# An mLSTM cell followed by a gated MLP: the first chunk's loads, masks and conversions are rearranged

## The chip, the cores and the metric

The kernel runs on one NeuronCore of a Trainium2 chip. The time is the device time of one execution in microseconds (us). The median of the kernel before is 486.15 us, of three runs between 485.81 and 486.62.

A core has five engines that run their own instruction streams and wait for each other through semaphores: TensorE (in the profile PE, and PEld for its weight loads), VectorE (DVE), ScalarE (ACT), GpSimd (POOL) and SyncE (SP), which here mostly issues loads. Matrix products land in PSUM; VectorE and ScalarE read it from there, GpSimd[...] only touches SBUF, the on-chip memory.

## The reference

There are 4 batches with 8 heads, a sequence of 768 and a head size of 40. Per head a matrix state `C` and a vector state `n` are updated at each step, with gates that are stabilised by a running maximum `m`; the output of all heads is one row of 320 numbers for a two-layer MLP.

```python
for t in range(S):
    m_new  = np.maximum(f_gate[:, :, t] + m, i_gate[:, :, t])
    f_stab = np.exp(f_gate[:, :, t] + m - m_new)
    i_stab = np.exp(i_gate[:, :, t] - m_new)
    m = m_new
    C = f_stab * C + i_stab * outer(v_t, k_t)
    n = f_stab * n + i_stab * k_t
    y[:, :, t] = sigmoid(o_t) * (C @ q_t) / np.maximum(np.abs(n @ q_t), 1.0)
x = y.transpose(0, 2, 1, 3).reshape(3072, 320)
h = x @ w_in                                  # 320 -> 2048
out = (h * sigmoid(1.702 * h)) @ w_out        # 2048 -> 320
```

## The kernel before

The sequence is cut into six chunks of 128 steps. Within a chunk the recurrence becomes a masked product: scores `k q`, times a weight `exp(a_s - m_t)` that is zero where s comes after t, times the values. Chunk 0 has no earlier state, so its attention begins as soon as keys, queries and gates are on the chip. While it runs, the weights `w_in` and `w_out` are loaded in 20 pieces (each 512 columns) and converted from their stored form by ScalarE ("A") and VectorE ("V"). Then the MLP of a chunk runs beside the attention of the next one.

The order of the loads, all issued by SyncE; `fetch(n)` loads piece n:

```python
def load_gates(w):
    for dst, src in ((f_sb, f_gate), (i_sb, i_gate)):
        dst[w] = ld.tile([BH, L], FP, tag="fi", bufs=4, name="fi")
        nc.sync.dma_start(out=dst[w], in_=src[:, :, w * L:(w + 1) * L].rearrange("b h s -> (b h) s"))

load_gates(0)
for what, n in (("kq", 0), ("kq", 1), (load_gates, 1), ("vo", 0), ("vo", 1), ("kq", 2), (fetch, 0), ("kq", 3),
                (fetch, 1), ("vo", 2), ("vo", 3), *((fetch, n) for n in range(2, 10))):
    ...
```

TensorE begins with dummy products, so that its array is busy until the first keys come; two buffers are cleared on ScalarE:

```python
def keep_busy(n, pool=ps_a, tag="a"):
    p_idle = pool.tile([128, W], FP, tag=tag, name="p_idle")
    for _ in range(n):
        T.matmul(p_idle, idle, idle.unsqueeze(1).to_broadcast([128, 4, 128]), start=True, stop=True)

keep_busy(8, ps_m, "m")
...
for t in (k_bl.rearrange("p j g c -> p (j g c)"), state.rearrange("p j a b -> p (j a b)")):
    A.copy(out=t, in_=idle[:, 0:1].to_broadcast(t.shape))
```

The conversion of a piece, the transposes of keys and queries, the weights and the scores of chunk 0. `ps_a` is a ring of four PSUM banks. `not_yet` holds -1e30 where s comes after t, and the first product of each bank adds it:

```python
def convert(n, engines="AV"):
    lo, hi, dst = bits[n][:, :, 0], bits[n][:, :, 1], pieces[n][0]
    dst_u = dst.bitcast(U32)
    if "A" in engines:
        A.activation(out=dst, in_=hi.bitcast(FP), func=AF.Abs)
        A.activation(out=lo, in_=lo, func=AF.Copy, scale=2.0 ** -29)
    if "V" not in engines:
        return
    V.tensor_scalar(...); V.tensor_scalar(...); V.scalar_tensor_tensor(...); V.tensor_tensor(...)   # cut

def transposes(w, b, which=slice(0, 2)):
    for bl, st, dst, name in ((k_bl, k_st, kT, "kT"), (q_bl, q_st, qT, "qT"))[which]:
        ...
        pt = ps_a.tile([128, NP, L], FP, tag="a", name="p_t")
        for p in range(NP):
            T.transpose(pt[:, p, :], st[:, h:h + 2, :]..., ident)
        if b == 0:
            keep_busy(1)
        A.copy(out=dst[w, b], in_=pt)

def weights(w, b):
    if w == 0:
        x = wt[w, b] = work.tile([L, NP, 2, L], FP, tag="wt", bufs=4, name="wt")
        for i in range(2):
            pw = ps_a.tile([L, NP, L], FP, tag="a", name="p_w")
            T.matmul(pw, ident_bf, not_yet.unsqueeze(1).to_broadcast([L, NP, L]), start=True, stop=False)
            for p in range(NP):
                h = b * H + 2 * p + i
                one = pick[:, h:h + 1].to_broadcast([3 * BH, L])
                T.matmul(pw[:, p, :], one, m3, start=False, stop=False)
                T.matmul(pw[:, p, :], a3, one, start=False, stop=(p == NP - 1))
            A.activation(out=x[:, :, i, :], in_=pw, func=AF.Exp)
        return
    ...

def scores(w, b):
    pw = [pool.tile([L, NP, L], FP, tag=tag, name="p_s") for _ in range(2)]      # pool: ps_a in chunk 0
    ...                                                                          # 8 products into two banks
    for i in range(2):
        V.tensor_tensor(out=wt[w, b][:, :, i, :], in0=pw[i], in1=wt[w, b][:, :, i, :], op=OP.mult)
```

The first chunk's sequence:

```python
gates(0)
...
transposes(0, 0)
weights(0, 0)
transposes(0, 1)
gates(1)
scores(0, 0)
weights(0, 1)
scores(0, 1)
gate_out(0); gate_out(1)
values(0, 0); values(0, 1)
transposes(0, 2)
convert(0, "A")
weights(0, 2)
seam(0, 0); seam(0, 1)
convert(0, "V")
scores(0, 2)
convert(1, "A")
transposes(0, 3)
weights(0, 3)
convert(1, "V")
scores(0, 3)
columns(0)
gate_out(2); gate_out(3)
scale(0, 0); scale(0, 1)
values(0, 2, states=True); values(0, 3, states=True)
full_rows(0, 0, 0); full_rows(1, 0, 0)      # first products with w_in, pieces 0 and 1
convert(2, "A")                             # piece 2: the last 64 rows of w_in, hidden blocks 0 to 3
seam(0, 2); full_rows(0, 1, 0); seam(0, 3); full_rows(1, 1, 0)
convert(2, "V")
convert(3)
convert(4)
...                                         # more full_rows, then the products with w_in_x (piece 2)
```

`seam` transposes a batch's output rows for the MLP, `gate_out` applies the output gate's tanh, `values` multiplies the weights by the values.

Of the kernel before, what the change touches and what calls it, by code (L numbers as in the profile page):

```python
# [12 lines left out]
OP = mybir.AluOpType  # L13
# [9 lines left out]
L = 128  # L23
# [11 lines left out]
def kernel(  # L35
# [12 lines left out]
    nc = tc.nc  # L48
    B, H, S, D = q.shape
# [4 lines left out]
    NP = H // 2  # L54
# [39 lines left out]
    def load_gates(w):  # L94
        for dst, src in ((f_sb, f_gate), (i_sb, i_gate)):
            dst[w] = ld.tile([BH, L], FP, tag="fi", bufs=4, name="fi")
            nc.sync.dma_start(out=dst[w], in_=src[:, :, w * L:(w + 1) * L].rearrange("b h s -> (b h) s"))

    def load(w, what, bs=slice(0, B)):
        hs = slice(bs.start * H, bs.stop * H)  # L100
# [66 lines left out]


    load_gates(0)
    for what, n in (("kq", 0), ("kq", 1), (load_gates, 1), ("vo", 0), ("vo", 1), ("kq", 2), (fetch, 0), ("kq", 3),  # L170
                    (fetch, 1), ("vo", 2), ("vo", 3), *((fetch, n) for n in range(2, 10))):
        if isinstance(what, str):
            load(0, what, slice(n, n + 1))
        else:
            what(n)
# [9 lines left out]
    def keep_busy(n, pool=ps_a, tag="a"):  # L185
        p_idle = pool.tile([128, W], FP, tag=tag, name="p_idle")
        for _ in range(n):
            T.matmul(p_idle, idle, idle.unsqueeze(1).to_broadcast([128, 4, 128]), start=True, stop=True)

    keep_busy(8, ps_m, "m")  # L190
    ident = const.tile([128, 128], FP, name="ident")
    make_identity(nc, ident)
    one1 = const.tile([BH, 1], FP, name="one1")
# [16 lines left out]
    a3 = const.tile([3 * BH, L], BF, name="a3")  # L210
    m3 = const.tile([3 * BH, L], BF, name="m3")
    state = const.tile([128, BH // 2, 2, D1], FP, name="state")
    for t in (k_bl.rearrange("p j g c -> p (j g c)"), state.rearrange("p j a b -> p (j a b)")):
        A.copy(out=t, in_=idle[:, 0:1].to_broadcast(t.shape))

    t1, t2, t4 = (const.tile([128, NH, DH], FP, name=f"t{i}") for i in (1, 2, 4))

# [2 lines left out]
    kT, qT, wt, ys, xT, gs, o_ps, p_c = {}, {}, {}, {}, {}, {}, {}, {}  # L220


    def convert(n, engines="AV"):

        lo, hi, dst = bits[n][:, :, 0], bits[n][:, :, 1], pieces[n][0]
        dst_u = dst.bitcast(U32)
        if "A" in engines:
            A.activation(out=dst, in_=hi.bitcast(FP), func=AF.Abs)
# [3 lines that stand above are left out]
        V.tensor_scalar(out=dst, in0=dst, scalar1=HI_MIN, scalar2=HI_MAX, op0=OP.max, op1=OP.min)  # L232
        V.tensor_scalar(out=dst_u, in0=dst_u, scalar1=3, scalar2=0x3FFFFFFF, op0=OP.logical_shift_left,
                        op1=OP.bitwise_and)
        V.scalar_tensor_tensor(out=dst_u, in0=hi, scalar=0xC0000000, in1=dst_u, op0=OP.bitwise_and,
                               op1=OP.bitwise_or)
        V.tensor_tensor(out=dst_u, in0=dst_u, in1=lo, op=OP.add)
# [59 lines left out]
    def transposes(w, b, which=slice(0, 2)):  # L297
        for bl, st, dst, name in ((k_bl, k_st, kT, "kT"), (q_bl, q_st, qT, "qT"))[which]:
            dst[w, b] = work.tile([128, NP, L], FP, tag=name, bufs=4, name=name)
            if w:  # L300
                V.transpose(out=dst[w, b].rearrange("p j t -> p (j t)"),
                            in_=bl[:, b * NP:(b + 1) * NP].rearrange("p j g c -> p (j g c)"))
                continue
            pt = ps_a.tile([128, NP, L], FP, tag="a", name="p_t")
            for p in range(NP):
                h = b * H + 2 * p
                T.transpose(pt[:, p, :], st[:, h:h + 2, :].rearrange("p a b -> p (a b)"), ident)
# [4 lines that stand above are left out]
    def spread(w):  # L312

        for b in range(B):
            x = wt[w, b] = work.tile([L, NP, 2, L], FP, tag="wt", bufs=4, name="wt")
            nc.sync.dma_start(out=x.rearrange("s p i t -> s (p i) t"),
                              in_=m_row[w][b * H:(b + 1) * H, :].unsqueeze(0).to_broadcast([L, H, L]))

    def weights(w, b):
        if w == 0:  # L320
            x = wt[w, b] = work.tile([L, NP, 2, L], FP, tag="wt", bufs=4, name="wt")
            for i in range(2):
                pw = ps_a.tile([L, NP, L], FP, tag="a", name="p_w")
                T.matmul(pw, ident_bf, not_yet.unsqueeze(1).to_broadcast([L, NP, L]), start=True, stop=False)
                for p in range(NP):
                    h = b * H + 2 * p + i
                    one = pick[:, h:h + 1].to_broadcast([3 * BH, L])
                    T.matmul(pw[:, p, :], one, m3, start=False, stop=False)
                    T.matmul(pw[:, p, :], a3, one, start=False, stop=(p == NP - 1))
                A.activation(out=x[:, :, i, :], in_=pw, func=AF.Exp)  # L330
            return
        x = wt[w, b].rearrange("s p i t -> s (p i) t")
        for h in range(H):
            A.activation(out=x[:, h, :], in_=x[:, h, :], func=AF.Exp, scale=-1.0,  # L334
                         bias=cols[w][:, b * H + h:b * H + h + 1])
        G.affine_select(out=x, in_=x, compare_op=OP.is_ge, fill=0.0, base=0, pattern=[[0, H], [1, L]],  # L336
                        channel_multiplier=-1)
        if w > 1 and b == 0:
            gates_out(w)

# [13 lines left out]
    def values(w, *bs, states=False):  # L354
        po, pi = {}, {}
        for b in bs:
            po[b] = ps_a.tile([L, H, D1], FP, tag="a", name="p_o")
            for p in range(NP):
                for i in range(2):
                    h = 2 * p + i  # L360
                    for t in HALVES:
                        T.matmul(po[b][t, h, :], wt[w, b][:, p, i, t], v_st[:, b * H + h, :], start=True, stop=True)
        for b in bs if w else ():
            pi[b] = ps_a.tile([L, H, D1], FP, tag="a", name="p_i")
            for p in range(NP):
                for t in HALVES:
                    T.matmul(pi[b][t, 2 * p:2 * p + 2, :].rearrange("p a b -> p (a b)"), qT[w, b][:, p, t],
                             state[:, b * NP + p].rearrange("p a b -> p (a b)"), start=True, stop=True)
        if states:
            for b in bs:  # L370
                scale_values(w, b)
        if states and w == 1:
            for b in bs:
                scale_state(w, b)
        elif states and w:

            new_states(w)
            for b in bs:
                scale_state(w, b)
        for b in bs:  # L380
            u = po[b]
            if w:
                u = work.tile([L, H, D1], FP, tag="u", name="u")
                g = cols[w][:, BH + b * H:BH + (b + 1) * H].unsqueeze(2).to_broadcast([L, H, D1])
                V.tensor_tensor(out=u, in0=pi[b], in1=g, op=OP.mult)
                V.tensor_tensor(out=u, in0=po[b], in1=u, op=OP.add)

            den = work.tile([L, H, 1], FP, tag="den", name="den")
            V.tensor_scalar(out=den, in0=u[:, :, D:D1], scalar1=-1.0, scalar2=1.0, op0=OP.mult, op1=OP.max)
            V.tensor_tensor(out=den, in0=u[:, :, D:D1], in1=den, op=OP.max)  # L390
            V.reciprocal(out=den, in_=den)
            z = eo[w][:, b * H:(b + 1) * H, :]
            V.scalar_tensor_tensor(out=z, in0=z, scalar=1.0, in1=u[:, :, 0:D], op0=OP.add, op1=OP.mult)
            y = ys[w, b] = work.tile([L, DM + 64], FP, tag="y", name="y")
            V.scalar_tensor_tensor(out=y[:, 0:DM].rearrange("p (h d) -> p h d", d=D), in0=z, scalar=0.5,
                                   in1=den.to_broadcast([L, H, D]), op0=OP.mult, op1=OP.mult)
            G.tensor_copy(out=y[:, DM:DM + 64], in_=y[:, DM - 64:DM])
# [21 lines left out]
    def scale(w, b):  # L419
        scale_values(w, b)  # L420
        scale_state(w, b)
# [238 lines left out]
    def gate_out(b):  # L660
        z = eo[0][:, b * H:(b + 1) * H, :]
        A.activation(out=z, in_=z, func=AF.Tanh, scale=0.5)
# [11 lines left out]
    V.tensor_reduce(out=pair, in_=ident[0:BH, 0:BH].rearrange("p (j two) -> p j two", two=2), axis=AX.X, op=OP.add)  # L674
    V.tensor_copy(out=half[0:BH], in_=par.unsqueeze(2).to_broadcast([BH, 2, 64]))
    transposes(0, 0)
    weights(0, 0)
    transposes(0, 1)
    gates(1)
    scores(0, 0)  # L680
    weights(0, 1)
    scores(0, 1)
    gate_out(0)
    gate_out(1)
    values(0, 0)
    values(0, 1)
    transposes(0, 2)
# [11 lines left out]
    columns(0)  # L699
    gate_out(2)  # L700
    gate_out(3)
    scale(0, 0)
    scale(0, 1)

# [16 lines left out]
    full_rows(0, 1, 0)  # L721
    seam(0, 3)
    full_rows(1, 1, 0)
    convert(2, "V")
    convert(3)
    convert(4)
    for j in range(2):
        for c in range(2):
            full_rows(j, c, 1)
# [132 lines left out]
```

## Time and profile before

| what | us |
|---|---|
| median time (three runs) | 486.15 |
| span of the profiled execution | 486.1 |
| TensorE busy | 480.6 |
| VectorE busy | 342.7 |
| ScalarE busy | 221.0 |
| GpSimd busy | 60.3 |
| first load issued | 0.81 |
| first transposes of keys start on TensorE | 5.02 |
| first scores start | 11.40 |
| first product with piece 2 of `w_in` starts | 36.17 |

A row of the order of time has the start, the duration (of the group from its first start to its last end), the engine, the line of the kernel, the operation, and what it writes and reads; a bracket tells how long the engine was idle before it, and what released it. A row of the table of stretches has each engine's busy time in that stretch. Ends of matrix products are modelled, so the durations of neighbours overlap, and the spacing of starts tells the pace better than a duration does.

### The profile page before, as it was taken

What the parts mean: (1) busy time and instruction counts of PE and PEld (TensorE: products, weight loads), DVE (VectorE), ACT (ScalarE), POOL (GpSimd) and SP (SyncE); (2) the same over time, 40 slices, a digit from 0 to 9 for tenths busy, and PEclk for the clock granted to TensorE, in tenths of its full rate; (3) what the DMA queues carried; (4) which work ended last, traced back from release to release, by engine and by line L of the source; (5) the groups of instructions that cost most, each with busy time, mean ns of one, the idle gap of its engine ahead of it and who ended that gap; (6) DMA issues with size and microseconds to landing.
All of it is one profiled execution on the core that took longest, in us unless ns stands there. A gap on an engine that the chain in (4) does not pass through costs nothing. (4 is left out here: it accounts for less than half of the span.)

```text
span 486.1 us, 10432 instructions
## 1 busy us (share of the span) xinstructions
PE 480.6 (99%) x4072; PEld 398.2 (82%) x4072; DVE 342.7 (70%) x853; ACT 221.0 (45%) x575; POOL 60.3 (12%) x101
## 2 busy tenths in 40 slices
PE   8999999999999999999999999999999999999997
PEld 5884457777779999787999877999977999977997
DVE  7798878887978965667766686696576786254831
ACT  6666764603559401467700465900364920255300
POOL 3020002520000430000331000232000120000000
DMA  8999589963996100997100796300393000000000
GB/s 121 188 270 347 66 202 188 171 81 70 169 202 73 11 28 30 155 209 80 8 29 1 119 253 75 32 28 3 77 261 28 1 14 17 28 1 0 1 27 28
DMA packets 175953, 44.87 MB, mean 92 GB/s; under 512 B 164352, under 2 KB 169504, under 8 KB 175904
## 3 DMA queue, kind: packets, MB, share of 16 engines
q1 hardware_dynamic: 175328, 43.55, 48.3%
q8 instruction: 32, 0.52, 0.5%
q10 hardware_dynamic: 576, 0.66, 0.4%
q14 instruction: 17, 0.14, 0.1%
HBM read 40.17 MB, written 4.01 MB: 91 GB/s over the span
## 5 line engine op out<-in xcount | busy, mean ns | idle before, releaser
L615 PE MATMUL p_out<-w_out_sb,g 128*128 128x160 f32 x480 | 69.8, 301 | 0.0
L615 PEld LDWEIGHTS p_out<-w_out_sb,g 128*128 128x128 f32 x480 | 66.3, 190 | 1.0
L405 ACT COPY xT<-p_x 128x384 f32<-128x384 f32 x24 | 10.8, 483 | 120.7 <-PE p_x L404 107.6
L526 DVE TENSOR_TENSOR g<-p_u,g 128x256 f32<-128x256 f32 x80 | 33.7, 425 | 44.6 <-PE p_u L518 35.0
L523 ACT COPY g<-p_u 128x256 f32<-128x256 f32 x120 | 43.1, 377 | 43.5 <-PE p_u L518 39.3
L530 ACT ACTIVATE g<-g 128x256 f32<-128x256 f32 x120 | 42.4, 425 | 39.7 <-DVE g L526 39.7
L336 POOL TENSOR_SCALAR_AFFINE_SELECT wt<-wt 128x1024 f32<-128x1024 f32 x20 | 22.8, 1138 | 239.3 <-ACT wt L334 236.9
L620 DVE TENSOR_TENSOR o_sb<-o_sb,p_out 128x160 f32<-128x160 f32 x70 | 21.4, 318 | 42.2 <-PE p_out L615 41.8
L334 ACT ACTIVATE wt<-wt,cols 128x128 f32<-128x128 f32 x160 | 47.9, 392 | 0.0
L518 PE MATMUL p_u<-xT,w_in_sb 128*128 128x256 f32 x160 | 38.9, 382 | 0.0
L518 PE MATMUL p_u<-xs,big 128*128 128x256 f32 x160 | 37.9, 379 | 0.0
L352 DVE TENSOR_TENSOR wt<-p_s,wt 128x512 f32<-128x512 f32 x48 | 30.4, 684 | 9.4 <-POOL wt L336 6.7
L546 PE MATMUL p_u<-xT,w_in_x 64*128 64x512 f32 x80 | 37.0, 602 | 0.0
L546 PE MATMUL p_v<-xT,w_in_x 64*128 64x512 f32 x80 | 37.0, 602 | 0.0
L566 PE MATMUL p_out<-w_out_sb,g 128*128 128x320 f32 x128 | 36.3, 436 | 0.0
L615 PE MATMUL p_out<-t,big 128*128 128x160 f32 x240 | 35.5, 301 | 0.0
L518 PEld LDWEIGHTS p_u<-xT,w_in_sb 128*128 128x128 f32 x160 | 29.6, 190 | 5.4 <-DVE o_sb L620 1.5
L518 PEld LDWEIGHTS p_u<-xs,big 128*128 128x128 f32 x160 | 30.0, 190 | 4.6 <-ACT g L523 0.2
L615 PEld LDWEIGHTS p_out<-t,big 128*128 128x128 f32 x240 | 33.3, 190 | 0.2
L566 PEld LDWEIGHTS p_out<-w_out_sb,g 128*128 128x128 f32 x128 | 23.8, 190 | 9.8 <-issue 0.5
L526 DVE TENSOR_TENSOR g<-p_v,g 128x256 f32<-128x256 f32 x80 | 29.9, 415 | 0.0
L546 PEld LDWEIGHTS p_v<-xT,w_in_x 64*128 64x128 f32 x80 | 14.2, 186 | 16.4 <-issue 16.0
(172 smaller groups left out, 862.0 us busy)
## 6 DMA issues: line engine op xcount, KB each, us to landing
wt<-m_row SPq DMA_DIRECT2D x20, 512.0 KB, 7.0
v_st<-in_v_dram SPq DMA_DIRECT2D x5, 640.0 KB, 8.9
eo<-in_o_gate_dram SPq DMA_DIRECT2D x5, 640.0 KB, 5.8
k_st<-in_k_dram SPq DMA_DIRECT2D x5, 640.0 KB, 11.4
out_dram<-o_sb SPq DMA_DIRECT2D x20, 160.0 KB, 1.8
big<-in_moe_w_in_dram SPq DMA_DIRECT2D x5, 512.0 KB, 6.8
k_bl<-in_k_dram SPq DMA_DIRECT2D x40, 64.0 KB, 2.8
q_bl<-in_q_dram SPq DMA_DIRECT2D x40, 64.0 KB, 2.8
```

Of the source, the lines that this page charges most:

```text
L334: A.activation(out=x[:, h, :], in_=x[:, h, :], func=AF.Exp, scale=-1.0, bias=cols[w][:, b * H + h:b * H + h + 1])
L336: G.affine_select(out=x, in_=x, compare_op=OP.is_ge, fill=0.0, base=0, pattern=[[0, H], [1, L]], channel_multiplier=-1)
L352: V.tensor_tensor(out=wt[w, b][:, :, i, :], in0=pw[i], in1=wt[w, b][:, :, i, :], op=OP.mult)
L405: A.copy(out=xT[w][:, :, b, :], in_=px)
L518: T.matmul(p[k][:, ts[t]], a[:, k // 2, k % 2 * 128:(k % 2 + 1) * 128], b, start=first, stop=True, skip_group_check=True)
L523: A.copy(out=g[k][i][:, ts[t]], in_=chain[k][:, ts[0]])
L526: V.tensor_tensor(out=g[k][i][:, ts[t]], in0=p[k][:, ts[pt]], in1=g[k][i][:, ts[t]], op=OP.add)
L530: A.activation(out=dst, in_=dst if src is None else src, func=AF.Gelu_apprx_sigmoid)
L546: T.matmul(p[k], w_in_x[r, k, :], x[r, 2, :], start=False, stop=True, skip_group_check=True)
L566: T.matmul(po, gs[w, f // 2][:, f % 2, b * L:(b + 1) * L], w_out_sb[:, f, :], start=(f == 0), stop=(f == NF - 1))
L615: T.matmul(po, a(f), b[:, f, :], start=(f == 0), stop=(f == NH - 1))
L620: V.tensor_tensor(out=dst, in0=x, in1=po, op=OP.add)
```

## The change

The gates of chunks 0 and 1 are loaded from ScalarE's queue, ahead of everything else there, so that SyncE's queue begins with the keys. One dummy product is left out. The clears of the two buffers leave the front of ScalarE's queue for later places. The keys of batch 1 are transposed before the weights of batch 0, to give TensorE work while the gates are computed. For batches 0 and 1 the mask is no longer added by TensorE: GpSimd writes zeros into the finished weights. Piece 2 (the 64 rows left over of `w_in`) is converted by VectorE in two halves, the second after pieces 3 and 4.

```diff
     def load_gates(w):
...
-            nc.sync.dma_start(out=dst[w], in_=src[:, :, w * L:(w + 1) * L].rearrange("b h s -> (b h) s"))
+            (nc.sync if w > 1 else nc.scalar).dma_start(
+                out=dst[w], in_=src[:, :, w * L:(w + 1) * L].rearrange("b h s -> (b h) s"))
...
     load_gates(0)
-    for what, n in (("kq", 0), ("kq", 1), (load_gates, 1), ("vo", 0), ("vo", 1), ("kq", 2), (fetch, 0), ("kq", 3),
+    load_gates(1)
+    for what, n in (("kq", 0), ("kq", 1), ("vo", 0), ("vo", 1), ("kq", 2), (fetch, 0), ("kq", 3),
...
-    keep_busy(8, ps_m, "m")
+    keep_busy(7, ps_m, "m")
...
-    for t in (k_bl.rearrange("p j g c -> p (j g c)"), state.rearrange("p j a b -> p (j a b)")):
+    def clear(t):
         A.copy(out=t, in_=idle[:, 0:1].to_broadcast(t.shape))
...
-    def convert(n, engines="AV"):
-        lo, hi, dst = bits[n][:, :, 0], bits[n][:, :, 1], pieces[n][0]
+    def convert(n, engines="AV", part=slice(0, 512)):
+        lo, hi, dst = bits[n][:, part, 0], bits[n][:, part, 1], pieces[n][0][:, part]
...
+    def causal(x, n):
+        G.affine_select(out=x, in_=x, compare_op=OP.is_ge, fill=0.0, base=0, pattern=[[0, n], [1, L]],
+                        channel_multiplier=-1)
...
-                T.matmul(pw, ident_bf, not_yet.unsqueeze(1).to_broadcast([L, NP, L]), start=True, stop=False)
+                if b > 1:
+                    T.matmul(pw, ident_bf, not_yet.unsqueeze(1).to_broadcast([L, NP, L]), start=True, stop=False)
...
-                    T.matmul(pw[:, p, :], one, m3, start=False, stop=False)
-                    T.matmul(pw[:, p, :], a3, one, start=False, stop=(p == NP - 1))
+                    T.matmul(pw[:, p, :], one, m3, start=(b < 2), stop=False)
+                    T.matmul(pw[:, p, :], a3, one, start=False, stop=(b < 2 or p == NP - 1))
                 A.activation(out=x[:, :, i, :], in_=pw, func=AF.Exp)
+                if b < 2:
+                    causal(x[:, :, i, :], NP)
...
     transposes(0, 0)
+    transposes(0, 1, slice(0, 1))
     weights(0, 0)
-    transposes(0, 1)
+    transposes(0, 1, slice(1, 2))
...
     gate_out(1)
+    clear(k_bl.rearrange("p j g c -> p (j g c)"))
...
     gate_out(3)
+    clear(state.rearrange("p j a b -> p (j a b)"))
...
-    convert(2, "V")
+    convert(2, "V", slice(0, 256))
     convert(3)
     convert(4)
+    convert(2, "V", slice(256, 512))
```

More of the change, by code (lines that the diff above doesn't have):

```diff
@@ L335, in weights @@
                          bias=cols[w][:, b * H + h:b * H + h + 1])
-        G.affine_select(out=x, in_=x, compare_op=OP.is_ge, fill=0.0, base=0, pattern=[[0, H], [1, L]],
-                        channel_multiplier=-1)
+        causal(x, H)
         if w > 1 and b == 0:
```

## The prediction

> **What bounds the kernel now.** First the page's busy shares, then the kernel cut into stretches of time, then TensorE's own order of time at the start, its waits, and the load queue.
>
> The page's first part, per engine busy us (share) and instructions:
>
> ```profile
> PE 480.6 (99%) x4072; PEld 398.2 (82%) x4072; DVE 342.7 (70%) x853; ACT 221.0 (45%) x575; POOL 60.3 (12%) x101
> ```
>
> TensorE (PE) has work for 480.6 of 486.1 us, so any gain must come out of the stretch where it is idle or doing work that the result doesn't need. The table of stretches says where that is:
>
> ```profile
> core 0: us, PE busy (x) PEld busy (x) DVE busy (x) ACT busy (x) POOL busy (x), PEclk, DMA share, GB/s
> 0.00:5.00 5.00, 3.60 (x8) 1.05 (x9) 3.64 (x13) 4.19 (x3) 2.89 (x12) 1.00 0.46 73
> 5.00:10.00 5.00, 4.91 (x24) 3.38 (x25) 3.80 (x16) 1.92 (x4) 1.72 (x5) 1.00 1.22 152
> ...
> 20.00:25.00 5.00, 4.64 (x50) 3.74 (x50) 4.54 (x9) 4.91 (x11) 0.00 (x0) 1.00 0.88 172
> 25.00:30.00 5.00, 4.97 (x88) 4.42 (x89) 4.62 (x13) 2.65 (x7) 2.91 (x5) 1.00 0.93 229
> ...
> 100.00:150.00 50.00, 49.91 (x361) 38.47 (x360) 41.09 (x93) 19.89 (x56) 3.48 (x7) 1.00 0.77 129
> ```
>
> In the first 5 us PE runs only eight dummy matmuls; after 30 us it is never idle for more than 0.1 us in a stretch until the tail. The DMA column shows the loads saturated (about 1) from 5 us. So the change, which touches only the first chunk, moves the point at which the dense stretch begins; if later stages can follow, the whole kernel shifts by that. TensorE's order of time (start, duration, line, and the idle time before it):
>
> ```profile
> 1.06 3.60 PE L188 MATMUL p_idle<-idle 128*128 128x512 bf16 x8 [1.06 <-DVE idle L182]
> 5.02 1.09 PE L307 MATMUL p_t<-ident,k_st 128*128 128x128 f32 x4 [0.37 <-DMA k_st<-in_k_dram]
> 5.90 0.63 PE L188 MATMUL p_idle<-idle 128*128 128x512 bf16 x1
> 6.60 1.09 PE L307 MATMUL p_t<-ident,q_bl 128*128 128x128 f32 x4
> ...
> 7.91 0.63 PE L324 MATMUL p_w<-xs 128*128 128x512 bf16 x1
> 8.33 0.31 PE L328 MATMUL p_w<-m,pick 96*128 96x128 bf16 x1
> ...
> 10.25 0.29 PE L328 MATMUL p_w<-m,pick 96*128 96x128 bf16 x1
> ...
> 10.43 0.61 PE L307 MATMUL p_t<-ident,k_st 128*128 128x128 f32 x4
> ```
>
> Two things set the pace: the first keys (PE waits 0.37 us for them at 5.02), and a slow array. Until 10.25 a 512-wide mask matmul takes 0.42 us from start to start (7.91 to 8.33) and a 128-wide one 0.107; four transposes take 0.88. After 10.25 the four transposes take 0.45 (10.43 to 10.88), and 512-wide ones 0.22. So PE works at half speed for 5.2 us with real work. The load queue of SyncE says why the keys come at 5.0:
>
> ```profile
> 0.81 0.40 SPq L97 DMA_DIRECT2D fi<-in_f_gate_dram  x1
> 1.26 0.41 SPq L97 DMA_DIRECT2D fi<-in_i_gate_dram  x1
> 1.72 0.42 SPq L105 DMA_DIRECT2D k_st<-in_k_dram  x1
> ```
>
> The keys' issue begins 0.91 us after the first gate's, and the keys land 3.2 us after their issue (the shortest time in the answer for k_st; 1.72 + 3.2 = 4.9).
>
> **What the Trainium skill says.** *TensorE: Matmul & The Clock Gate*, Part 1: the array starts at half clock and is released after one sufficiently busy window of 3413 ns; the windows run freely, so the moment varies between runs. The trace agrees in kind (half speed to 10.25, full speed after) and fits in size: 10.25 is 5.2 us after 5.02, so one window at most was spoilt. Part 4 of that page says that transposes don't count as busy in the same way; this trace can't tell. *DMA: Bandwidth & Descriptors*, "Issuing engines are not separate DMA queues": a second issuing engine saves only issue time. The trace agrees so far as it goes: an issue costs 0.41 us of SyncE, and there are four gate loads. *ScalarE: Activation LUTs*, "What ACT_TABLE_LOAD costs": 1283 ns a load; the trace has 1.28.
>
> **Part by part.**
>
> Gate loads on ScalarE. Two issues leave SyncE ahead of the first keys: 0.91 us. First keys land at about 4.0, and everything behind them in the saturated stream about 0.9 us sooner. The next gates leave SyncE too (4.52 to 6.3), which only helps issue, as DMA is the limit there. ScalarE spends 4 x 0.45 = 1.8 us on issues and 1.28 on its table, and is ready at 3.9; its first copy is wanted at about 5.2. That is possible only because the two clears (1.90 and 1.28 us) leave the front.
>
> Keep-busy 8 to 7: the dummies end about 0.43 sooner, near 4.2, and the keys are there at 4.0. The first transposes start at 4.2 in place of 5.02: 0.8 us gained, without a gap.
>
> Second keys sooner. PE in sequence, cold, 4 transposes 0.88, dummy 0.43: keys 4.22-5.1, dummy 5.53, queries (landing 5.4) 6.4, dummy 6.83, second keys (landing 1.89 + 4.7 = 6.6) 7.7. This fills the time in which the gates' arithmetic finishes (GpSimd ended it at 6.97), so the weights aren't waited for.
>
> Masks of two batches off PE. Four 512-wide matmuls: two cold at 0.42 and two warm at 0.22, 1.28 us of PE. Instead GpSimd masks 512 elements four times: between 0.29 us for 128 elements and 1.1 for 1024 in the trace, about 0.65 each. GpSimd does nothing from 6.97 to 18.01, so it has the room; each mask sits between an exponential and VectorE's product, which waits for the scores anyway. With the array cold throughout: weights 7.7-9.4, second queries to 10.3, scores at 10.3 where before it was 11.40. So 1.1 us gained. Batch 1's masks (0.43 us) are not gained: scores of batch 1 reuse the two banks that VectorE must empty (1.29 us for the two products after the first scores end); before, the masked weights filled 12.5 to 13.93 and the products ended at 13.96. Without the masks PE gets there 0.4 to 0.5 us before VectorE is done, and waits.
>
> The clears (1.90 and 1.28 us) go to ScalarE's idle times before 18.18 (2.83 us) and 29.05 (1.35 us, for a DMA). They just fit: 0.
>
> Piece in halves. VectorE converts 256 of the 512 columns of piece 2 (2.44 us whole, so about 1.3 with overhead), then pieces 3 and 4, which end 1.1 us sooner against the rest; the second half is wanted only at 43.08. It costs four more instruction overheads, some 0.2 us of VectorE, and gives PE room to come earlier: without it, piece 4 has about 2 us of slack (done 37.85, used at 39.9).
>
> Sum with the clock released as before: 0.8 + 0.3 = 1.1 us. The clock is the large unknown. Now PE has no gap from 1.06 on, so the release can come at the window that closed at 10.25 - 3.41 = 6.84. Cold work between 6.84 and 10.25 takes half the time: up to 1.7 us more. Data then limits: second queries land at 8.1, ScalarE and GpSimd chains add 0.3, so about 1.3 to 1.5 us are left, and 2.5 in all.
>
> **The rivals.**
>
> A. Clock as late as before: 1.1 us, 485.0 us. For it: transposes are 2.6 us of PE between 4.2 and 7.7. Chance 0.4.
>
> B. Clock released a window sooner: 2.5 us, less what the weights' pieces and later loads hold back; 483.8. For it: the gap before 5.02 is the only real one, and it goes. Chance 0.45.
>
> C. Transposes really don't count. Then more of them between 6.84 and 10.25 (second keys, second queries: 1.76 us) spoil the window that released the clock before; full speed comes at 13.66 and costs up to 1.7 us: 486.5. Chance 0.15.
>
> D. Later stages don't follow. Loads move by only 0.9 us. Piece 2 of w_in arrived about 29.0 (ScalarE waited 1.35 us for it), and its conversion has 3.2 us of slack before 36.17; around 100 us, in VectorE's and TensorE's order of time, the last piece of w_out is converted at 101.2 and used at about 102.2, 1.0 of slack plus the 0.9 us. So gains up to about 1.9 pass whole, and 2.5 might lose some tenths. This is in B's number.
>
> E. GpSimd's masks come late and PE waits for products: the masks end at most 0.65 us after an exponential, and the products wait for scores that end later; a tenth or two at worst.
>
> **Range and chances.** 0.4 x 485.0 + 0.45 x 483.8 + 0.15 x 486.5 = 484.7. The change looks fitted to the arrival of the keys, and the halved piece makes sense only if PE really comes near 2 us early, so I lean to B: 484.4 us. Range 483.1 to 485.8: B whole at the bottom, A with a loss of 0.7 at the top. Two per cent is 9.7 us, more than the whole time before the first score, so within 2% is nearly sure: faster 0.02, same 0.97, slower 0.01.
>
> **What would show it.** Right: first transposes of keys at 4.0 to 4.3 with no wait on DMA; scores of batch 0 at 10.3 (A) or near 8.8 (B) in place of 11.40; 128-wide weight matmuls at 0.107 spacing throughout the first weights (A) or 0.055 (B); a new wait of PE on VectorE's product of 0.4 to 0.6 us before the scores of batch 1; the eight matmuls with w_in_x that started at 36.17 now at 35.0 (A) or 33.9 (B), and the end earlier by the same. Wrong: keys landing later than 4.4, because the gates' packets share the engines; ScalarE's first copy later than PE's transposes; waits on weights' pieces before 45 us; a shift at 38 us that is smaller at 110 us.

## The result and the profile after

The changed kernel takes 489.50 us (median of six runs, 487.54 to 490.88) against 486.32 us for the kernel before in the same session (six runs, 485.81 to 487.17). The ratio is 1.0063, with a 95% interval of 1.0040 to 1.0086. It is slower by 3.2 us. The prediction was 484.4 us, with a range that ended at 485.8.

The page's first part of the kernel after:

```profile
PE 477.8 (98%) x4067; PEld 396.8 (82%) x4067; DVE 343.7 (71%) x857; ACT 220.2 (45%) x575; POOL 62.6 (13%) x105
```

TensorE has five instructions less than before (four masks and a dummy), as meant, and is busy for 477.8 us instead of 480.6. Yet the time rose: what was taken away has turned into idle time. The table of stretches of the kernel after (columns as in the prediction's) says where:

```profile
0.00:5.00 5.00, 3.79 (x10) 1.54 (x11) 2.65 (x9) 1.28 (x1) 2.36 (x10) 1.00 0.70 101
5.00:10.00 5.00, 3.86 (x32) 2.70 (x31) 4.01 (x18) 2.29 (x5) 2.25 (x6) 1.00 1.49 158
10.00:15.00 5.00, 3.44 (x51) 2.92 (x49) 4.33 (x10) 4.03 (x8) 2.49 (x4) 1.00 1.21 202
...
30.00:100.00 70.00, 70.00 (x438) 43.06 (x437) 59.40 (x113) 43.82 (x92) 9.89 (x13) 1.00 0.93 195
```

From 30 us on TensorE is as dense as before. Between 5 and 15 us it is idle for 2.7 us. TensorE's order of time names the places:

```profile
1.06 3.17 PE L190 MATMUL p_idle<-idle 128*128 128x512 bf16 x7 [1.06 <-DVE idle L184]
4.38 1.09 PE L311 MATMUL p_t<-ident,k_st 128*128 128x128 f32 x4
...
7.11 0.63 PE L311 MATMUL p_t<-ident,k_st 128*128 128x128 f32 x4 [0.25 <-DMA k_st<-in_k_dram]
8.60 0.23 PE L338 MATMUL p_w<-m,pick 96*128 96x128 bf16 x1 [0.86 <-DVE m L251]
...
10.25 1.16 PE L361 MATMUL p_s<-qT,kT 40*128 40x128 f32 x16
13.97 1.16 PE L361 MATMUL p_s<-qT,kT 40*128 40x128 f32 x16 [1.56 <-DVE wt L363]
...
36.21 1.99 PE L749 MATMUL p_h<-xT,w_in_x 64*128 64x512 f32 x8
```

The keys' transposes start at 4.38, 0.64 us sooner than in the first profile of before, without a wait. Then come two waits that the kernel before doesn't have: 0.86 us for the gates' running maximum `m` ahead of the first weights, and 1.56 us for VectorE's product ahead of the scores of batch 1. The products with `w_in_x` start at 36.21.

VectorE's order of time in the kernel after shows what made both:

```profile
3.58 0.41 DVE L258 TENSOR_TENSOR_SCAN f_run<-one,fi 32x128 f32<-32x128 f32 x1
5.67 0.28 DVE L260 TENSOR_TENSOR st<-fi,f_run 32x128 f32<-32x128 f32 x1 [1.68 <-DMA fi<-in_i_gate_dram]
...
9.91 0.41 DVE L258 TENSOR_TENSOR_SCAN f_run<-one,fi 32x128 f32<-32x128 f32 x1
10.35 0.62 DVE L260 TENSOR_TENSOR st<-fi,f_run 32x128 f32<-32x128 f32 x1
11.01 0.73 DVE L266 TENSOR_TENSOR_SCAN m_run<-one,m_end,st 32x128 f32<-32x128 f32 x1
...
12.70 0.62 DVE L285 TENSOR_SCALAR dec_in<-pair,both 32x16 f32<-32x16 f32 x1
13.24 1.27 DVE L363 TENSOR_TENSOR wt<-p_s,wt 128x512 f32<-128x512 f32 x2
```

At 5.67 VectorE has waited 1.68 us for chunk 0's input gate, and everything behind it is late. From 9.91 it computes the gates of chunk 1, which stand ahead of the products in its order. They end at about 13.2, so the products start 1.8 us after the scores of batch 0 have ended (10.25 + 1.16 = 11.4), and TensorE waits for the banks that the products empty.

ScalarE's and then SyncE's queue in the kernel after (issue time, duration, load):

```profile
0.80 0.46 ACTq L97 DMA_DIRECT2D fi<-in_f_gate_dram  x1
1.29 0.59 ACTq L97 DMA_DIRECT2D fi<-in_i_gate_dram  x1
```

```profile
0.81 0.44 SPq L106 DMA_DIRECT2D k_st<-in_k_dram  x1
```

The input gate is issued at 1.29, practically the 1.26 of before. In the trace of before it landed 1.7 us after its issue; here it takes 4.3 us, with the keys, issued at 0.81, under way. Whether the keys are the reason is tested below.

Those are the waits of the profiled execution, which took 487.54 us at a mean granted clock of 1.000. It is the fastest of the six. The others have spans of 487.5 to 489.2 us at a clock of 0.990 to 0.993: in them full speed was taken back for a while. One trace below, of a kernel with one dummy more, shows when.

### The profile page after: what moved, and what is told of

It reads as the page before. It is cut to its first block, busy times and chain, and to the rows that moved or that the text cites. A ratio compares the mean times of both kernels' runs of the same rounds, so it can differ in the third digit from the quotient of the medians.

```text
span 485.8 us, 10430 instructions
## 1 busy us (share of the span) xinstructions
PE 477.8 (98%) x4067; PEld 396.8 (82%) x4067; DVE 343.7 (71%) x857; ACT 220.2 (45%) x575; POOL 62.6 (13%) x105
## 5 line engine op out<-in xcount | busy, mean ns | idle before, releaser
L325 POOL TENSOR_SCALAR_AFFINE_SELECT wt<-wt 128x1024 f32<-128x1024 f32 (+1 forms) x24 | 25.2, 1054 | 236.3 <-ACT wt L346 187.1
L361 PE MATMUL p_s<-qT,kT 40*128 40x128 f32 x384 | 25.7, 280 | 1.9 <-DVE wt L363 1.6
```

Source lines behind the costliest of these rows:

```text
L361: T.matmul(pw[i][:, p, :], kT[w, b][r, p, :], qT[w, b][r, p, :], start=True, stop=True)
```

## The experiments

In each, "before" is the median of the kernel before on the same chip, beside these runs: 485.99, 485.84, 485.88 and 485.97 us in the four sessions, of about 30 runs each. The span is 1.7 us shorter than the time in every run.

**The kernel before, once more** (`before_again`, no edit).

> The kernel before once more, for its trace: the runs measured since have spans of 484.1 to 484.8 us, where the profiled one had 486.1. Theory (the trace was not typical): full speed comes [...]sooner than at 10.25, near 6.8, so that the first scores start 1.7 us sooner, at about 9.7, and the products with w_in_x at about 34.4. Rival: the start is the same (11.40 and 36.17), and the 1.8 us are lost elsewhere.

485.79 us, span 484.1. Its stretch from 10 to 15 us:

```profile
10.00:15.00 5.00, 4.82 (x85) 3.92 (x82) 3.74 (x12) 2.02 (x5) 0.00 (x0) 1.00 1.19 194
```

TensorE's order of time, and then VectorE's:

```profile
5.13 0.63 PE L307 MATMUL p_t<-ident,k_st 128*128 128x128 f32 x4 [0.49 <-DMA k_st<-in_k_dram]
...
9.32 1.16 PE L350 MATMUL p_s<-qT,kT 40*128 40x128 f32 x16
11.86 1.75 PE L350 MATMUL p_s<-qT,kT 40*128 40x128 f32 x16
...
34.48 1.99 PE L733 MATMUL p_h<-xT,w_in_x 64*128 64x512 f32 x8
```

```profile
3.84 0.28 DVE L256 TENSOR_TENSOR st<-fi,f_run 32x128 f32<-32x128 f32 x1
...
9.24 0.28 DVE L256 TENSOR_TENSOR st<-fi,f_run 32x128 f32<-32x128 f32 x1
9.56 0.47 DVE L262 TENSOR_TENSOR_SCAN m_run<-one,m_end,st 32x128 f32<-32x128 f32 x1
...
10.99 0.22 DVE L281 TENSOR_SCALAR dec_in<-pair,both 32x16 f32<-32x16 f32 x1
11.13 1.27 DVE L352 TENSOR_TENSOR wt<-p_s,wt 128x512 f32<-128x512 f32 x2
```

In this execution four transposes take 0.63 us already at 5.13, against 1.09 in the profile that the prediction rests on: the array is at full speed five microseconds sooner, and `w_in_x` comes at 34.48 and not at 36.17. Its span is the usual one (most spans of before lie at 484.0 to 484.7). The first profile, with 486.1, was of an execution whose array woke late: it took 487.83 us, 1.7 above the median of 486.15, and only the span of 486.1 stood beside that median. So "full speed a window sooner" was mostly no longer there to be won. The row also gives the yardstick for the kernel after: products at 11.13 against 13.24, scores of batch 1 at 11.86 without a wait against 13.97, TensorE busy for 4.82 of the five microseconds against 3.44. And VectorE's operations on chunk 1's gates, which are the same in both kernels, took 0.28, 0.47 and 0.22 us here, 0.62, 0.73 and 0.62 there.

**The kernel after, again** (`after_again` timed; `after_trace` and `after_trace2` one traced execution each; no edit).

> The changed kernel once more, for the granted TensorE clock of each run. Theory (clock): TensorE's two new waits in the first chunk, 0.86 us for the gates and 1.56 us for VectorE's products, let the clock fall back for some microseconds in most runs; then the median is 489 to 490 us, the mean granted clock 0.990 to 0.993 in the long runs and 1.000 in the short ones (about 487.5). Rival (work): the 3 us are time that the engines wait for each other later; then long runs have the same clock as short ones.

> The changed kernel once more, for a trace of a run with a mean clock below 1.000. Theory (clock falls back in the waits): between 8 and 25 us there is a stretch of 3.4 to 10 us in which the 128-wide products are 0.107 us apart in place of 0.055, and it begins after one of the two waits of TensorE (0.86 us before the weights, 1.56 us before the scores of batch 1); span 486.5 to 490. Rival: the slow stretch lies elsewhere in the kernel.

> The changed kernel once more, for a trace with a mean clock below 1.000; expected as for after_trace: a stretch of 3.4 to 10 us of half speed that begins after one of the two waits of TensorE, span 486.5 to 490, against the same loss elsewhere in the kernel.

`after_again`: 489.82 us (median of the five below), ratio 1.0066 (1.0032 to 1.0100). Its spans, each with its clock: 484.9 at 1.000, 486.6 at 0.996, 488.1 at 0.993, 488.3 at 0.990, 490.1 at 0.986. (A sixth, at a mean clock of 0.65, is left out.) The two traced executions gave 487.51 and 487.11 us, both at 1.000, both with the 1.56 us wait, and with 0.8 and 0.5 us ahead of the weights; `after_trace` missed its expectation of a fall of the clock. The longer the span, the lower the clock; at 1.000 the kernel is only 0.8 to 1.7 us behind before's 484.1. Two losses have to be told apart: the waits themselves, and the clock.

**The waits filled with work that nobody needs** (`fill`; `fill_second` has only the second addition).

```diff
     transposes(0, 1, slice(0, 1))
+    keep_busy(4, ps_m, "m")
     weights(0, 0)
...
     weights(0, 1)
+    keep_busy(7, ps_m, "m")
     scores(0, 1)
```

> The changed kernel with eleven more dummy products on TensorE: four before the weights of batch 0, seven before the scores of batch 1, where it waits anyway. Theory (clock): the array stays busy, the clock doesn't fall, and adding work makes the kernel faster: 486.0 to 487.5 us, clock 1.000 in every run. Rival (work): nothing gained, 489 to 490 us, or worse by the 0.2 to 0.5 us that the dummies overlap the end of the waits.

> The changed kernel with seven matmuls on constants only where TensorE waits 1.56 us before the second batch's scores; the wait of 0.86 us before the first weights is left. Theory A (the later, longer wait alone makes the clock fall back): all runs at a clock of 1.000, spans 485.3-486.4, median 487.2-487.7 us. Theory B (the two waits together do it, as idle time of one stretch): some of the runs show 0.990-0.996 and spans over 487, median 488-489.5 us.

`fill`: 487.47 us, ratio 1.0029 (1.0019 to 1.0039), all ten runs at 1.000. `fill_second`: 487.19 us, 1.0023 (1.0014 to 1.0032), all ten at 0.999 to 1.000. TensorE's order of time in `fill_second`:

```profile
8.28 0.23 PE L338 MATMUL p_w<-m,pick 96*128 96x128 bf16 x1 [0.58 <-DVE m L251]
...
11.93 1.68 PE L190 MATMUL p_idle<-idle 128*128 128x512 bf16 x7
13.64 1.16 PE L361 MATMUL p_s<-qT,kT 40*128 40x128 f32 x16
```

Seven matmuls on constants make the kernel some 2 us faster. They don't bring the scores of batch 1 forward to speak of (13.64, against 13.52 to 13.97 in the three traces of the kernel after at full clock); they only keep the array busy. So the clock is worth 2.0 to 2.6 us: the kernel after is 3.2 and 3.8 us behind the kernel before beside it, `fill_second` 1.2. And of the two waits it is enough to fill the second: with the first left (0.58 us in this trace), the clock held.

**The eighth dummy back** (`after_8`), and taken from the kernel before (`before_7`): `keep_busy(8, …)` for 7, and the reverse.

> The changed kernel with eight dummy products again, nothing else. Eight cold ones fill 3.4 us, seven only 3.0. Theory (two causes): full speed comes at about 4.5 in most runs, but the input gate lands as late as before (near 5.5) and the wait before the scores of batch 1 stays at 1.5 us, so that the span is 485.3 to 485.8 at clock 1.000 and the time 487.0 to 487.5; if the clock still falls back in that wait, some runs are 1 to 4 us above this. Rival (the missing dummy is the whole loss): 485.4 to 486.

> The kernel before with seven dummy products in place of eight. Theory (the eighth dummy completes the window that releases the clock): full speed comes later in most runs, as in the first trace of before, 487.0 to 487.8 us. Rival (the window's place decides, not the dummy): unchanged, 485.8.

`after_8`: 489.57 us, ratio 1.0078 (1.0061 to 1.0094), all four runs at 0.993. `before_7`: 485.96 us, ratio 1.0009 (1.0000 to 1.0018), eight of twelve spans at 484.1 to 484.8. The dummy isn't the cause of the loss. (Four of the spans of `before_7` are 485.3 to 485.6, where before beside it has one of 29 above 484.7, so seven may be a little few for an early release; that isn't shown.) `after_8` is where the fall can be read in a trace. The stretches around its wait:

```profile
11.00:14.00 3.00, 1.44 (x24) 1.15 (x24) 2.89 (x8) 2.09 (x5) 1.60 (x3) 1.00 1.26 190
14.00:17.00 3.00, 3.00 (x54) 2.83 (x56) 1.71 (x4) 1.49 (x1) 0.00 (x0) 0.64 1.28 212
17.00:20.00 3.00, 3.00 (x39) 2.92 (x38) 2.57 (x10) 0.26 (x1) 0.24 (x1) 0.50 0.99 229
20.00:23.00 3.00, 3.00 (x27) 2.45 (x25) 1.35 (x4) 2.73 (x6) 0.24 (x1) 0.72 0.84 152
23.00:26.00 3.00, 3.00 (x35) 2.67 (x34) 2.69 (x5) 3.00 (x7) 0.00 (x0) 1.00 0.86 224
```

and TensorE's order of time there:

```profile
13.87 1.21 PE L361 MATMUL p_s<-qT,kT 40*128 40x128 f32 x16 [1.56 <-DVE wt L363]
15.01 3.64 PE L373 MATMUL p_o<-v_st,wt 128*64 128x41 f32 x64
18.59 1.11 PE L311 MATMUL p_t<-ident,k_st 128*128 128x128 f32 x4
```

The granted clock, third number from the end of a line, is 1.00 up to 14 us, in a stretch in which TensorE worked 1.44 of 3 us, then 0.64, 0.50 and 0.72, then 1.00 again. At 0.50 four transposes take 1.11 us for 0.63. Not everything doubles: the 64 products with the values take 3.6 us here (15.01 to 18.59) and 2.3 in `before_again` (13.54 to 15.80). Nor does this number show the half speed of a kernel's start: in the first profile of before it stands at 1.00 from 5 to 10 us, where 128-wide products are 0.107 us apart. A mean clock of 1.000 says only that full speed was not lost later. The lost share is 3 x (0.36 + 0.50 + 0.28) = 3.4 us of clock, that is 6.8 us at half speed. A mean of 0.993 over 488 us says the same: 0.007 x 488 = 3.4. The span grows by less: it is 487.7 to 488.1 in the four runs, and 484.9 to 485.8 in the four of the kernel after at 1.000. A part of the difference is seen: from 15 to 25 us TensorE is never idle in `after_8`, and idle for 0.61 us in the kernel after. Notably, the fall comes after the wait, when TensorE is busy again.

**Where the late gate comes from.** `i_gate_first` issues only chunk 0's input gate from SyncE, ahead of the keys; `i_gate_first_8` has eight dummies besides. `loads_as_before` puts all the loads back and leaves the rest of the change. `loads_clears` is the opposite: the kernel before with nothing but the loads on ScalarE and the clears moved.

```diff
# i_gate_first
-            (nc.sync if w > 1 else nc.scalar).dma_start(
+            (nc.sync if w > 1 or (w == 0 and src is i_gate) else nc.scalar).dma_start(
# loads_as_before
-            (nc.sync if w > 1 else nc.scalar).dma_start(
+            nc.sync.dma_start(
-    load_gates(1)
-    for what, n in (("kq", 0), ("kq", 1), ("vo", 0), ...
+    for what, n in (("kq", 0), ("kq", 1), (load_gates, 1), ("vo", 0), ...
```

> The changed kernel, but the input gate of chunk 0 is the first load on SyncE, ahead of the keys, and only the other three gate loads go by ScalarE. Theory (gates behind keys): the gate, which landed at 5.67 us behind the first keys, lands by 3.5; the keys move back 0.45 us, the weights of batch 0 start without a wait by 8.3 and the products of VectorE about 1.5 us sooner, so that the wait before the scores of batch 1 shrinks from 1.56 to 0.3 to 0.6 us; time 484.7 to 485.8 us. Rival: the gates of chunk 1, still behind the keys, hold VectorE as long, and the wait stays above 1 us: 486 us or more.

> i_gate_first with eight dummy products in place of seven. There the keys come at 4.78 and the seven end 0.55 us earlier. Theory (the gap delays the release of the clock): without the gap full speed comes at 6.4 to 7 as in the changed kernel, the first scores start near 9.6, and the time falls by 0.5 to 1 us to 484.4 to 485.0. Rival (data is the limit, second queries and VectorE's products): 485.2 to 485.6, unchanged.

> The changed kernel with the loads as they were: all gates by SyncE, those of chunk 0 ahead of the keys, those of chunk 1 after the keys of batch 1. Theory: with seven dummies there is a gap of some 0.8 us before the keys, but the gates aren't late; first scores at 10.2 to 10.8, a wait of about 0.5 us before the scores of batch 1; 485.2 to 486.3 us, clock 1.000. Rival (the loss is in GpSimd's masks, not in the loads): 488 us or more.

> The kernel before with only the gates' loads on ScalarE and the two clears moved out of their way: eight dummies, masks on TensorE, keys in the old order, piece 2 whole. Theory (gates behind keys): the input gate lands at 5.3 to 5.7, the weights start at 8.3 to 8.6 in place of 7.23, VectorE's first products at 13 or later in place of 11.13, and TensorE waits for them: 486.8 to 488 us. Rival (keys 0.8 us sooner outweigh it): 485.0 to 485.8.

| kernel | us | ratio to before (95%) | wait before weights | wait on products before scores of batch 1 |
|---|---|---|---|---|
| i_gate_first | 485.44 | 0.9992 (0.9983 to 1.0001) | none | none |
| i_gate_first_8 | 485.36 | 0.9991 (0.9985 to 0.9998) | none | 0.56 |
| loads_as_before | 486.32 | 1.0007 (0.9999 to 1.0016) | none | none |
| loads_clears | 486.84 | 1.0023 (1.0014 to 1.0031) | 1.1 | none |

One load moved from one queue to the other is worth 4.4 us (489.82 and 485.44 in the same session), and the clock is at 0.999 to 1.000 in every run of the first three. The move changes the queue and the place beside the keys at once. But the second load of ScalarE's queue in `i_gate_first`, issued at 1.3 together with the keys, lands after 2.6 us; so standing second in that queue doesn't make the 4.3 by itself. In `loads_as_before` the rest of the change, with the gate on time, is 0.3 us behind before, which its interval doesn't set apart from nothing.

The "none" of `i_gate_first` and `loads_as_before` can't be set beside the 0.56: in these two profiles the array is still at half speed (128-wide products 0.107 us apart) until 9.97 and 9.88, the scores of batch 0 come late, and the products are ready in time. At full speed, in `i_gate_first_8`, a wait is left:

```profile
11.77 1.16 PE L361 MATMUL p_s<-qT,kT 40*128 40x128 f32 x16 [0.56 <-DVE wt L363]
```

VectorE's order of time in `i_gate_first_8` shows the gate in time again (landing 1.7 to 1.9 us after its issue), at the price of 0.3 us on the keys (first transposes at 4.69):

```profile
3.86 0.28 DVE L260 TENSOR_TENSOR st<-fi,f_run 32x128 f32<-32x128 f32 x1
```

and in `loads_clears`, where it lands 3.6 us after its issue, late without anything else of the change:

```profile
5.02 0.28 DVE L260 TENSOR_TENSOR st<-fi,f_run 32x128 f32<-32x128 f32 x1 [1.07 <-DMA fi<-in_i_gate_dram]
```

with, among TensorE's waits of `loads_clears` (total us, times, longest):

```profile
PE p_w L338 <- DVE m L251: 1.1, 1, 1.1
```

So the loads, with the clears moved, cost about 1 us by themselves. The expectation had VectorE's products at 13 or later; they start at 11.58, and TensorE doesn't wait for them. Yet three of the eighteen runs lost some clock (0.996, spans of 486.8 to 487.0), without a wait of 1.56 us; where they lost it, no trace shows. The expectation that the eighth dummy would make `i_gate_first_8` half a microsecond faster missed (485.36 against 485.44).

**The masks.** Both kernels have the masks of batches 0 and 1 on TensorE again, `i_gate_first_masks_pe` with the gate on time, `after_masks_pe` with the gate late; both otherwise as the kernel after.

```diff
-                if b > 1:
-                    T.matmul(pw, ident_bf, not_yet..., start=True, stop=False)
+                T.matmul(pw, ident_bf, not_yet..., start=True, stop=False)
...
-                if b < 2:
-                    causal(x[:, :, i, :], NP)
```

> i_gate_first, but the masks of batches 0 and 1 are added by TensorE again (four 512-wide products) and GpSimd masks nothing there. Theory (TensorE is the limit once the gates are in time): slower by what the four products take less the wait for VectorE, 0.5 to 1.0 us, 486.0 to 486.5. Rival (VectorE's chain is the limit and TensorE would wait anyway): within 0.2 us of 485.44.

> The changed kernel with the masks of batches 0 and 1 on TensorE again; the input gate of chunk 0 stays late (ScalarE's queue). Theory A (two causes: the late gate sets VectorE back by some 1.8 us, and GpSimd's masks beside the second chunk's gate arithmetic stretch it by another 1.0 us): that arithmetic takes 2.4 us again, the wait before the second batch's scores falls from 1.56 to 0.3 us or less, the granted clock stays at 1.000 in nearly all runs, and the median falls from 489.5 to 486.5-487.2 us. Theory B (the late gate alone makes the wait, the masks cost nothing): a wait of 1.2 us or more stays, most runs show a clock of 0.993 and spans of 487 and more, median 489-490 us.

With the gate on time it made 485.63 us, ratio 0.9993 (0.9985 to 1.0002): 0.2 us from `i_gate_first`. Taking four mask matmuls off TensorE is worth almost nothing. With the gate late it made 486.82 us, ratio 1.0012 (1.0004 to 1.0021), all twelve runs at 0.999 or more: 0.85 us behind before, where the changed kernel is 3.2 and 3.8 behind. The scores of batch 1 start at 13.04 without a wait. VectorE's order of time in `after_masks_pe`:

```profile
10.39 0.28 DVE L260 TENSOR_TENSOR st<-fi,f_run 32x128 f32<-32x128 f32 x1
10.71 0.47 DVE L266 TENSOR_TENSOR_SCAN m_run<-one,m_end,st 32x128 f32<-32x128 f32 x1
...
12.14 0.22 DVE L285 TENSOR_SCALAR dec_in<-pair,both 32x16 f32<-32x16 f32 x1
12.29 1.27 DVE L361 TENSOR_TENSOR wt<-p_s,wt 128x512 f32<-128x512 f32 x2
```

The gate arithmetic starts at 9.95 here and at 9.91 in the kernel after, but ends 0.95 us sooner. The reason stands in GpSimd's order of time in the kernel after:

```profile
10.20 1.27 POOL L325 TENSOR_SCALAR_AFFINE_SELECT wt<-wt 128x512 f32<-128x512 f32 x2 [1.40 <-ACT wt L340]
12.66 1.22 POOL L325 TENSOR_SCALAR_AFFINE_SELECT wt<-wt 128x512 f32<-128x512 f32 x2 [1.19 <-ACT wt L340]
```

The three stretched operations (10.35, 11.01, 12.70) begin while a mask runs; the ones in between, from 11.78 to 12.67, take what they always take. In the Trainium skill, *SBUF — State Buffer*, "Who interferes with whom", VectorE shares one pair of ports with GpSimd, and an operation of VectorE with two inputs in SBUF, or in a two-port mode, contends for it. The runs agree so far: the first two have two inputs in SBUF and are stretched by 0.34 and 0.26 us, while the products at 13.24, with one input in PSUM, begin beside a mask and take their usual 1.27 us for two. The third, stretched by 0.40, has one input of 32 x 16; whether it runs in a two-port mode, and which port was held, no trace shows. In `i_gate_first_8` masks stretch chunk 1's gates as well (0.40 us for 0.15 and 0.64 for 0.28), but these start 1.8 us sooner there (8.09), and the wait behind them is 0.56.

**VectorE's order** (`gates_split`). From `i_gate_first_8`: four operations on chunk 1's gates, which only the transposed columns need, go behind the first products.

```diff
+        if w == 1:
+            late.extend((m, st, m_run, a, end))
+            return
+        gates_rest(w, m, st, m_run, a, end)       # the two subtractions into st, both, dec_in
...
     scores(0, 0)
+    gates_rest(1, *late)
     weights(0, 1)
```

> As i_gate_first_8 (eight matmuls on constants, input gate of chunk 0 first on SyncE's queue), and of the second chunk's gate arithmetic four operations, which only the transposed columns need, move behind the products of the first scores on VectorE. Theory A (what is left of the wait before the second batch's scores is VectorE's gate arithmetic ahead of the products): the products start at 10.3-10.6 instead of 11.04, the wait of 0.56 us before the scores falls to 0.1 or less, and the span falls by 0.4-0.6 us to 483.1-483.3, time 484.8-485.0 us. Theory B (the scores' second buffers or the weights of batch 1 come last there, or a later wait takes the gain): the scores of batch 1 start within 0.2 us of 11.77, time 485.2-485.5 us.

485.98 us, ratio 1.0002 (0.9994 to 1.0010); the profiled span is 483.9 against 483.6. VectorE's order of time, and then TensorE's:

```profile
10.51 1.29 DVE L371 TENSOR_TENSOR wt<-p_s,wt 128x512 f32<-128x512 f32 x2 [0.63 <-POOL wt L333]
...
13.30 1.27 DVE L371 TENSOR_TENSOR wt<-p_s,wt 128x512 f32<-128x512 f32 x2
```

```profile
11.33 1.47 PE L369 MATMUL p_s<-qT,kT 40*128 40x128 f32 x16
...
14.62 1.02 PE L381 MATMUL p_o<-v_st,wt 128*64 128x41 f32 x28 [0.24 <-DVE wt L371]
```

The first products start 0.53 us sooner (11.04 in `i_gate_first_8`), now held by GpSimd's mask, and the scores of batch 1 start at 11.33 instead of 11.77. But the operations moved back now stand ahead of the second products, which come at 13.30 instead of 13.03, and the values behind them at 14.62 instead of 14.37. Of this 0.19 us is a later start of batch 0's scores (9.24 for 9.05), which the edit doesn't touch; even so nothing is left of the gain three microseconds later, and the time lies above both expectations. Nothing tried beats `i_gate_first_8`, which is 0.5 us faster than before.

## Why the prediction was wrong

*Two issues off SyncE, keys 0.9 us sooner, seven dummies, no gap.* Right but for 0.2 us: the keys landed at 4.2 and not at 4.0, and the transposes start at 4.19 to 4.38 in six traces of kernels with these loads and seven dummies, the prediction's "4.2", with no wait or 0.2 us of one.

*"This fills the time in which the gates' arithmetic finishes (GpSimd ended it at 6.97), so the weights aren't waited for."* This is the step that failed. It took the gates' arithmetic from the kernel before as a fixed time. But the input gate's landing moved from 1.7 to 4.3 us after its issue. VectorE's operation on it moved from 3.84 to 5.67, GpSimd ended at 8.81, and TensorE waited 0.86 us. The prediction's list of things that would show it wrong had the sign reversed: "keys landing later … because the gates' packets share the engines". The keys came on time, and the gates were late behind them. The prediction had cited that a second issuing engine saves only issue time, and then reckoned with that time alone: it never asked when the gates, no longer ahead of the keys, would land. `loads_clears` and `i_gate_first` measure this step: about +1 us by itself, and 4.4 us between the changed kernel and one with that load ahead of the keys again. The difference is the meeting of two things: the late gate without GpSimd's masks costs 0.85 us (`after_masks_pe`), the masks with the gate on time nothing, and only both make the wait of 1.56 us behind which the clock falls.

*Rival E: "a tenth or two at worst" for GpSimd's masks; "0.4 to 0.5 us" of waiting before the scores of batch 1.* Wrong in size, and by the wrong path. The masks weren't late. They slowed VectorE's gates of chunk 1 by 0.95 us, and these stand ahead of the products. With the late gate this made 1.56 us. With the gate on time and eight dummies the wait was 0.56, close to what was predicted. Of the 1.1 us that earlier keys and the masks' removal were to bring, the masks' share is within 0.2 us of nothing.

*The clock.* Rivals A, B and C all concern the moment of its first release. The array did reach full speed without another gap, as B had it, but so does the kernel before in most executions; the one profile that was read was an exception. That took away the 1.3 to 1.5 us that B put on the clock. That the clock could be lost again at 14 us was in no rival. It is the largest term: 2.0 to 2.6 us.

*The clears cost 0.* Right as far as seen: with the old masks and a gate on time, nothing of them shows, and they were never tried alone. *The halved piece.* TensorE never came early enough for its slack to matter; it wasn't tried alone either. *Rival C* (transposes don't count): not seen. *The chances*: within 2% was right, though not for the reason given: the first score came at 11.40 us, and 9.7 us is less than that.

Sum, each against before beside it: the changed kernel is 3.2 and 3.8 us behind; the waits at full clock are 1.2 of this (`fill_second`), the clock is the rest. As a difference this closes by itself, but the spans bear it out: the changed kernel is 0.8 to 1.7 us behind 484.1 at a clock of 1.000, and 3.4 to 5.1 at 0.990 to 0.993.

## What to carry to other kernels

A small load that starts a long chain belongs ahead of the large ones; a second queue saved an issue here, and the load arrived later all the same. When work is moved to an idle engine, look at what its neighbour does in the same microseconds, not only at whether the engine has room. And one profile of the kernel before isn't enough where the clock's first release decides: take its span beside the spans of its other runs before reading gains from it.

## What was not expected of the hardware

- **A wait of 1.56 us was enough to lose the clock.** The Trainium skill, *TensorE: Matmul & The Clock Gate*, "Why this matters for your kernels", asks for no idle gaps over about 3 us; here the stretch with the 1.56 us wait (1.44 of 3 us busy) was followed by 6.8 us at half speed. The measurement decides. It happens in most runs and not in all, which the free-running windows of the prediction would explain; no run shows where a window begins. In `fill_second`, where the array has no such gap, it happened in none of ten runs. How much idle time is enough isn't settled, nor is it the idle share alone: in the trace of `after_masks_pe` TensorE is busy for only 1.69 of the 3.5 us from 5.14 to 8.64, but idle in shorter pieces, and none of twelve runs lost clock.
- **A load of 16 KB landed 4.3 us after its issue behind the keys, and after 1.7 us ahead of them**, issued at the same moment (1.29 and 1.26). The runs show that its place decides, not by what rule the packets take turns.
- **A GpSimd mask stretched small VectorE operations that began beside it by 0.25 to 0.40 us each**, even one of 32 x 16 elements (0.62 for 0.22 us).
